# A linear-attention and expert kernel: the table of row numbers is built in SBUF by one-hot matmuls instead of by scatters to DRAM

## The chip, the cores and the metric

The kernel runs on one core of one Trainium2 chip. The metric is device time in microseconds (us), smaller is better; the time before is the median of three runs. A profile is one execution recorded by the hardware profiler; its span is shorter than the device time by what lies around it.

## The reference

Two stages follow each other. The first is a recurrence over 768 positions for 4 batches and 8 heads of width 48:

```python
for t in range(S):
    state = alpha[:, :, t, :, None] * state + np.einsum('bhd,bhe->bhde', k[:, :, t], v[:, :, t])
    y[:, :, t] = np.einsum('bhd,bhde->bhe', q[:, :, t], state)
```

Its output, as 3072 rows of 384 numbers, goes through a layer of 8 experts, one expert per row, with a gate that lets some rows pass unchanged:

```python
do_compute = x @ w_skip > 0
xc = x[do_compute]
logits = xc @ w_gate
e_idx = np.argmax(logits, axis=1)
probs = softmax(logits)                      # largest one is the weight of the row
for e in range(8):
    mask = e_idx == e
    y[mask] = gate_w[mask, None] * (np.maximum(xc[mask] @ w1[e], 0) @ w2[e])
out = x.copy();  out[do_compute] = xc + y    # w1: 384 x 1024, w2: 1024 x 384
```

## The kernel before, in words

The program has one order of instructions for each engine, written out by hand: what stands earlier in the text is issued earlier on its engine, and an engine waits in order. Engines wait for each other by semaphores where data require it.

**Attention, steps 0 to 23.** The 3072 rows are 24 tiles of 128 (tile i: batch i % 4, positions from 128 * (i // 4)). A pair j is the tiles 2j and 2j + 1. `step(i)` does for tile i, or one tile ahead: `scores` (L328, q times k, of tile i + 1), `turn_k` (L341, transposed k, of tile i + 1, up to tile 19), `causal` (L334, DVE: scores below the mask into `st`), `inter` (L358, q times state), `outer` (L384, k times v for the next state, up to tile 19), `intra` (L367, `st` times v), `rows` (L406 and L415: the output turned into rows, of the tile before), `store` (SP: rows to `out`, of two tiles before). The decays come from two scans per pair on DVE, `suffix` (L282) and `prefix` (L300), two pairs ahead; GpSimd multiplies k and q by them (L311, L307) and scales the state (L399). `inspect` (L318, ScalarE) checks that the decays lie within bounds.

**Routing.** Tiles are taken in groups (`GROUPS`). At the end of a group `logits` (L436) multiplies its outputs by the gate weights, `logits_turn` (L446) transposes, and `route` does on DVE: the row maximum, the difference, which expert and whether the row is on (`mg`, a 0/1 matrix of rows by experts), the exponentials on ScalarE and their sum. `rank` (L496 to L502) counts with triangular matmuls how many rows of the same expert stand before a row. Groups from tile `LATE` = 18 on count downwards from slot 255, the others upwards from 0, so that an expert's 256 slots hold early rows below and late rows above. `slots` picks the rank by `mg`. `tick` advances these small operations a few at a time between the large ones.

**The table.** For each tile `scatter` (L526, an indirect DMA issued by GpSimd) writes, for its 128 rows, row number and exponential sum (8 bytes) to `xs` in DRAM at slot 3072 * expert + rank. `xs` is cleared at step 1 (`clear`). `metas` (L643, SP) reads the first 256 slots of each expert back into SBUF once every scatter has landed. `fetch_rows` (L549, indirect DMA from GpSimd) gathers the 256 rows of an expert from `out` by these numbers. An empty slot holds a number out of bounds and is skipped; the buffer was cleared before.

**Expert 0's first rows.** To begin expert 0 before the last rows are in DRAM, `early_rows` (step 21) reads its table as it stands, step 22 gathers those rows into `xr0`, and the rows from tile 18 on reach expert 0 by matmuls: `slots` makes a one-hot matrix `hot` per late tile (L521), `late_parts` splits the tile's rows into two float parts (L558, L559), and `late_rows` (L566) multiplies the two, summing into the PSUM tile `x01`; `early_turn` adds the gathered ones. `split_x` turns both halves into the float parts that the experts use. `attention_end` holds this order.

**Experts.** For each expert, `up` (L686, four blocks of 36 matmul records in two), `down` twice (L701), `turn` of the next expert's gathered rows (L671) between the two, `put` (L708 and an indirect DMA, L710: rows times gate plus input, written to their place in `out`). Weights come by `fetch` on SP's queue, four DMAs each for w1 and w2, and `split` makes the two float parts of them (ScalarE L618, DVE L620). Gathers run three experts ahead. `must_redo` (expert 5) checks whether the shortcuts held; if not, a general path runs at the end.

Instructions of the late stage take over SBUF and PSUM of the attention stage, each waiting until the tile that it overlays is free.

Of the kernel before, what the change touches and what calls it, by code (L numbers as in the profile page):

```python
# [44 lines left out]
BIG = float(1 << 20)  # L45
OFF = 1 << 20
GMAX = 4
GROUPS = ((0, 4), (4, 8), (8, 12), (12, 16), (16, 18), (18, 21), (21, 23), (23, 24))
LATE = 18
TABLE = 16  # L50
# [12 lines left out]
class Kernel:  # L63
# [12 lines left out]
    def constants_first(self):  # L76
# [3 lines left out]
        dram = self.ctx.enter_context(tc.tile_pool(name="dram", bufs=1, space=DRAM))  # L80
        self.dram = dram
        self.xs = dram.tile([E * N, 2], F32, name="xs")
# [26 lines left out]
    def constants_late(self):  # L109
# [13 lines left out]
        base_i = const.tile([1, E], I32, name="base_i")  # L123
        nc.gpsimd.iota(base_i, pattern=[[N, E]], base=0, channel_multiplier=0)
        self.base_row = const.tile([P, 1, E], BF16, name="base_row")
        nc.gpsimd.memset(self.base_row, 0.0)
        nc.gpsimd.tensor_copy(self.base_row[0:1, 0, :], base_i)
# [5 lines left out]
        self.slot = const.tile([P, NT, 1], U32, name="slot")  # L133
        self.idg = const.tile([P, NT, 2], F32, name="idg")
        nc.gpsimd.iota(self.idg[:, :, 0:1].bitcast(I32).rearrange("p (c b) w -> p c b w", b=B),
                       pattern=[[P, C], [S, B], [0, 1]], base=0, channel_multiplier=1)
# [5 lines left out]
        self.empty = const.tile([E, CAP, 2], F32, name="empty")  # L142
        nc.gpsimd.memset(self.empty, 0.0)
        nc.gpsimd.iota(self.empty[:, :, 0:1].bitcast(I32), pattern=[[0, CAP]], base=OFF, channel_multiplier=0)

    def constants_slots(self):

        nc, const = self.nc, self.const
        slots_i = const.tile([P, P], I32, name="slots_i")
        nc.gpsimd.iota(slots_i, pattern=[[1, P]], base=P, channel_multiplier=0)  # L150
        self.slots1 = const.tile([P, P], F32, name="slots1")
        nc.gpsimd.tensor_copy(self.slots1, slots_i)
# [5 lines left out]
    def clear(self):  # L158

        self.nc.sync.dma_start(out=self.xs.rearrange("(e n) w -> e n w", e=E)[:, :CAP, :].rearrange("e n w -> e (n w)"),  # L160
                               in_=self.empty.rearrange("e n w -> e (n w)"))

    def clear_late(self):

        for i in range(LATE + 3, NT):
            row = self.row(i)
            self.nc.sync.dma_start(out=self.out[row:row + P, :], in_=self.xr0[:, 0, :])
# [1029 lines left out]
```

## Time and profile before

| | |
|---|---|
| Device time, median of 3 | 296.95 us (296.1 to 298.43) |
| Profiled execution: device time | 296.78 us |
| Its span | 295.0 us |
| Busy: PE / DVE / ACT / POOL | 268.8 / 210.0 / 159.4 / 132.4 us |
| Bytes moved by DMA | 55.22 MB |

PE is TensorE, PEld its weight loads, DVE VectorE, ACT ScalarE, POOL GpSimd, SP the engine that issues most DMAs. Times in the profile are counted from the start of the span. "L701" is line 701 of the kernel; names such as `ps_o<-w2h,hh` are output and inputs without buffer numbers. The chain of waits follows the work that ended last back to its releasers; "issue" in it is time in which the profile shows no wait. A matmul in four passes is listed by its records, so counts can be twice those of the text.

### The profile page before, as it was taken

The page shows a single profiled execution, that of the slowest core. Times are in us where ns is not written, and L with a number is a line of the kernel's source. Part 1 is how long each engine was busy: PE and PEld are TensorE (multiplying, and loading weights), DVE is VectorE, ACT ScalarE, POOL GpSimd, SP SyncE. Part 2 cuts the span into 40 slices and gives each one's busy share as a digit, 9 for nine tenths or more (in the row PEclk, how much of TensorE's full clock was granted, in tenths as well). Part 3 has the DMA queues.
Part 4 walks back from the last instruction along what each step waited for, and adds up shares of the span by engine and source line. Part 5 has one row for each costly group of instructions (what it writes and reads, how often), then busy time and mean ns, then how long its engine had stood idle before and what let it go on. Part 6 is the DMA issues. An engine that isn't in the chain of part 4 may idle for free.

```text
span 295.0 us, 7438 instructions
## 1 busy us (share of the span) xinstructions
PE 268.8 (91%) x2933; PEld 246.7 (84%) x2933; DVE 210.0 (71%) x376; ACT 159.4 (54%) x388; POOL 132.4 (45%) x141
## 2 busy tenths in 40 slices
PE   8967999999879989999947999999999999999980
PEld 8856888888758768779926999999999999999980
DVE  7999899898795959853525585785758878585720
ACT  8897657567537547542623364745636366354600
POOL 8847567888767665537134503205050230202011
PEclk9999999999999968999996999999999999999996
DMA  5999999799999924023069728578382865815000
GB/s 171 296 265 269 288 287 280 137 255 166 191 290 274 302 86 107 6 60 81 3 199 339 253 78 300 192 221 296 112 306 78 282 232 180 290 36 224 4 29 19
DMA packets 29690, 55.22 MB, mean 187 GB/s; under 512 B 6600, under 2 KB 13312, under 8 KB 29648
## 3 DMA queue, kind: packets, MB, share of 16 engines
q1 hardware_dynamic: 26704, 49.60, 59.8%
q0 software_dynamic: 2944, 5.07, 4.7%
q8 instruction: 25, 0.41, 0.7%
q14 instruction: 17, 0.14, 0.2%
HBM read 47.80 MB, written 8.50 MB: 191 GB/s over the span
## 4 chain that ended last, share of the span: by engine, by line
PE 76%; DMA 7%; DVE 6%; ACT 4%; issue 3%; POOL 1%; POOLq 0%; SPq 0%; DVEq 0%
PE ps_o L701 21%; PE ps_h L686 21%; PE ps_s L328 7%; PE ps_y L367 6%; PE ps_y L358 4%; PE ps_k L406 4%; PE ps_v L384 3%; DMA xs<-idg,slot 3%; PE ps_k L341 3%; DVE sfx L282 3%; PE ps_n L436 2%; DMA xr<-out_dram,meta 2%; PE ps_x L671 2%; DVE pfx L300 1%; DVE st L334 1%
## 5 line engine op out<-in xcount | busy, mean ns | idle before, releaser
L710 POOL DMA_INDIRECT out_dram<-o,meta x16 | 16.1, 1003 | 98.9 <-DVE o L708 98.3
L690 ACT ACTIVATE hh<-ps_h 128x512 fp32r<-128x512 f32 x32 | 19.1, 598 | 48.0 <-PE ps_h L686 48.0
L701 PE MATMUL ps_o<-w2h,hh 128*128 128x384 f32 x128 | 43.9, 343 | 0.0
L701 PE MATMUL ps_o<-w2l,hh 128*128 128x384 f32 x128 | 43.4, 339 | 0.2 <-DVE w2l L620 0.2
L691 DVE SCALAR_TENSOR_TENSOR hl<-ps_h,hh 128x512 fp32r<-128x512 f32 x32 | 22.1, 691 | 29.6 <-ACT hh L690 29.6
L701 PE MATMUL ps_o<-w2h,hl 128*128 128x384 f32 x128 | 43.1, 337 | 0.0
L334 DVE COPY_PREDICATED st<-mask,ps_s 128x1024 f32<-128x1024 uint8 x24 | 31.6, 1315 | 5.4 <-PE ps_s L328 5.4
L311 POOL TENSOR_TENSOR qk<-qk,sfx 112x512 f32<-112x512 f32 x24 | 28.0, 1183 | 14.1 <-DVE dec L296 2.9
L686 PE MATMUL ps_h<-xh,w1h 128*128 128x256 f32 x192 | 33.7, 284 | 0.4 <-ACT xh L585 0.4
L307 POOL TENSOR_TENSOR qk<-qk,pfx 112x512 f32<-112x512 f32 x23 | 26.8, 1180 | 15.8 <-DVE pfx L300 15.8
L686 PE MATMUL ps_h<-xh,w1l 128*128 128x256 f32 x192 | 33.4, 283 | 0.0
L620 DVE TENSOR_TENSOR w2l<-raw,w2h 128x512 fp32r<-128x512 f32 x48 | 31.4, 683 | 2.7 <-ACT w2h L618 2.7
L620 DVE TENSOR_TENSOR w1l<-raw,w1h 128x512 fp32r<-128x512 f32 x48 | 31.3, 705 | 0.0
L318 ACT ACTIVATE junk<-dec 112x512 bf16<-112x512 f32 x48 | 30.6, 638 | 0.8
L371 ACT COPY xt<-ps_y 112x256 f32<-112x256 f32 x48 | 15.5, 374 | 28.5 <-PE ps_y L367 28.5
L618 ACT CAST w1h<-raw 128x512 fp32r<-128x512 f32 x48 | 26.8, 626 | 5.5 <-DMA raw<-in_w_dram 5.5
L618 ACT CAST w2h<-raw 128x512 fp32r<-128x512 f32 x48 | 27.9, 615 | 2.8 <-DMA out_dram<-x 2.8
L328 PE MATMUL ps_s<-qk 64*128 64x128 f32 (+1 forms) x384 | 28.9, 291 | 0.4 <-POOL qk L307 0.4
L549 POOL DMA_INDIRECT xr<-out_dram,meta x18 | 19.7, 1093 | 21.2 <-issue 10.0
L367 PE MATMUL ps_y<-st,v 128*64 128x128 f32 x384 | 28.2, 280 | 0.9 <-issue 0.9
L300 DVE TENSOR_TENSOR_SCAN pfx<-dec,ps_t 112x1040 f32<-112x1040 f32 (+1 forms) x14 | 28.2, 2011 | 1.2
L686 PEld LDWEIGHTS ps_h<-xh,w1h 128*128 128x128 f32 x192 | 28.0, 191 | 0.5 <-ACT xh L585 0.5
(161 smaller groups left out, 555.0 us busy)
## 6 DMA issues: line engine op xcount, KB each, us to landing
raw<-in_w_dram SPq DMA_DIRECT2D x64, 384.0 KB, 4.8
qk<-in_qk_dram SPq DMA_DIRECT2D x20, 384.0 KB, 9.3
dec<-in_dec_dram SPq DMA_DIRECT2D x24, 198.0 KB, 6.9
v<-in_v_dram SPq DMA_DIRECT2D x12, 384.0 KB, 7.7
out_dram<-x SPq DMA_DIRECT2D x24, 192.0 KB, 6.9
qk<-in_qk_dram SPq DMA_DIRECT2D x8, 192.0 KB, 5.7
out_dram<-xr SPq DMA_DIRECT2D x3, 192.0 KB, 7.4
xs<-idg,slot POOLq DMA_INDIRECT x24, 7.6
```

Source lines behind the costliest of these rows:

```text
L300: nc.vector.tensor_tensor_scan(w["pfx"][:PD, s], w["dec"][:PD, s], self.top[:PD].to_broadcast([PD, s.stop - s.start]), 1.0, ALU.mult, ALU.max)
L307: (eng or self.nc.gpsimd).tensor_tensor(w["qh"][:PD], w["qh"][:PD], w["pfx"][:PD], ALU.mult)
L311: (eng or self.nc.gpsimd).tensor_tensor(w["kh"][:PD], w["kh"][:PD], w["sfx"][:PD], ALU.mult)
L318: self.nc.scalar.activation(out=self.junk[:PD], in_=dec, func=AF.Relu, scale=scale, bias=bias, accum_out=self.odd[:PD, n, i:i + 1])
L328: nc.tensor.matmul(ps[:, h, p * P:(p + 1) * P], lhsT=kh[r, p, :], rhs=qh[r, p, :], start=True, stop=True)
L334: self.nc.vector.copy_predicated(w["st"], self.mask, w["ps"])
L367: nc.tensor.matmul(self.place(i, h, p), lhsT=w["v"][:, o:o + 64], rhs=w["st"][:, h, p * P:(p + 1) * P], start=(i < B and p < 2), stop=(p > ...
L618: nc.scalar.copy(out=hi[:, s], in_=raw[:, s])
L620: eng.tensor_tensor(lo[:, s], raw[:, s], hi[:, s].bitcast(F32), ALU.subtract)
L686: nc.tensor.matmul(ps[:, u, :], lhsT=a[:, k, f * P:(f + 1) * P], rhs=b[:, k, :], start=(n == 0), stop=(n == len(order) - 1))
L691: nc.vector.scalar_tensor_tensor(out=hl, in0=ps, scalar=0.0, in1=hh.bitcast(F32), op0=ALU.max, op1=ALU.subtract)
L701: nc.tensor.matmul(ps, lhsT=a[:, f, js], rhs=b[:, f, :], start=(n == 0), stop=(n == 3 * FT - 1))
```

## The change

The table of row numbers no longer goes through DRAM. Each row gets a one-hot vector of 128 slots (`hots`) and, per expert and half of the slots, six small numbers (`vals`): 1, tile number and position within it, and the exponential sum in three bf16 parts (`facts`). A matmul per tile, hots transposed times vals, summed over tiles, puts them in PSUM at partition = slot: `table`. `ids` makes row numbers of it, with an out-of-bounds number for a slot that does not hold exactly one row.

- `scatter`, `clear`, `metas` and `gates` go, with their constants. `sums` and `marks` make `facts`, `hots` and `vals`: on GpSimd for the groups ending at 4, 8, 12 and 16 (seven operations at each odd step, `run_jobs`), on DVE (the sums on GpSimd) for tiles 16 to 19, and on GpSimd for the late groups at the end.
- The late part starts at tile 20, not 18: groups are 0-4, 4-8, 8-12, 12-16, 16-20, 20-23 and 23-24.
- Ranks and slots of an early group stand right after `scores` and `turn_k`, ahead of the scans of the step; before, they came after `inter`, behind the scans.
- `early_rows` (step 21) multiplies the 20 early tiles' table and gathers expert 0's early rows at once. `early_turn` moves from `attention_end` to the start of step 23. Late stores need not wait for that gather any more (`apart`).
- `late_table` runs after expert 0's first up block: the four late tiles' table is added, row numbers and gates of all experts are made, and the gathers of experts 1, 0 and 2 follow.
- Buffers for gathered rows exist from the start and are cleared at steps 15, 21 and 22; `clear_late` moves from step 14 to 17 and covers four tiles. `inspect` runs three tiles ahead, not four. The order at the end of the attention is another.

The diff, cut to its core:

```diff
-GROUPS = ((0, 4), (4, 8), (8, 12), (12, 16), (16, 18), (18, 21), (21, 23), (23, 24))
-LATE = 18
+GROUPS = ((0, 4), (4, 8), (8, 12), (12, 16), (16, 20), (20, 23), (23, 24))
+LATE = 20
...
-        for i in range(LATE + 3, NT):
+        for i in range(LATE, NT):
...
+    def sums(self, g, eng):
...
+        yield eng.tensor_copy(part(3), w["sum"])
+        yield eng.tensor_tensor(rest[:, :, 0:1], w["sum"], part(3), ALU.subtract)
+        yield eng.tensor_copy(part(4), rest[:, :, 0:1])
+        yield eng.tensor_tensor(part(5), rest[:, :, 0:1], part(4), ALU.subtract)
+
+    def marks(self, g, eng, eng_hot):
...
+            yield eng.tensor_scalar(out=up, in0=w["s"], scalar1=float(P), scalar2=None, op0=ALU.is_ge)
+            yield eng.tensor_scalar(out=s, in0=up, scalar1=-float(P), scalar2=None, op0=ALU.mult)
+            yield eng.tensor_tensor(s, s, w["s"], ALU.add)
+            yield eng.tensor_tensor(half[:, :, 1, :], mg, up.to_broadcast([P, n, E]), ALU.mult)
+            yield eng.tensor_tensor(half[:, :, 0, :], mg, half[:, :, 1, :], ALU.subtract)
...
+        for t in range(n):
+            yield eng_hot.tensor_scalar(out=hots[:, t, :], in0=slots, scalar1=s[:, t, :], scalar2=None, op0=ALU.is_equal)
...
+        yield eng.tensor_tensor(vals.rearrange("p t j e w -> p t (j e) w"), mg.unsqueeze(3).to_broadcast(shape),
+                                self.facts[:, g0:g1, :].unsqueeze(2).to_broadcast(shape), ALU.mult)
+
+    def table(self, groups, ps):
+
+        tiles = [(self.grp[g0], t) for g0, g1 in groups for t in range(g1 - g0)]
+        for n, (w, t) in enumerate(tiles):
+            self.nc.tensor.matmul(ps, lhsT=w["hots"][:, t, :], rhs=w["vals"][:, t].rearrange("p j e w -> p (j e w)"),
+                                  start=(n == 0), stop=(n == len(tiles) - 1))
+
+    def ids(self, out, tab):
...
+        nc.vector.tensor_scalar(out=b, in0=col(0), scalar1=1.0, scalar2=float(OFF), op0=ALU.not_equal, op1=ALU.mult)
+        nc.vector.scalar_tensor_tensor(out=a, in0=col(1), scalar=float(P), in1=col(2), op0=ALU.mult, op1=ALU.add)
+        nc.vector.tensor_tensor(out, a, b, ALU.add)
...
     def early_rows(self):
...
-        self.meta0 = self.late.tile([P, NB, 2], F32, name="meta0")
-        ins = nc.sync.dma_start(out=self.meta0, in_=self.slot_rows(0))
-        self.after(ins.ins, "xs")
-        self.early = [ins.ins.name]
+        ps = self.bank[:, P + 32 * GMAX:][:, 0:NB * E * TABLE]
+        self.table([g for g in GROUPS if g[0] < LATE], ps)
+        self.rowtab = self.late.tile([P, NB, E, TABLE], F32, name="rowtab")
+        nc.scalar.copy(out=self.rowtab.rearrange("p j e w -> p (j e w)"), in_=ps)
+        first = self.late.tile([P, NB, 1], U32, name="first")
+        self.ids(first, self.rowtab[:, :, 0:1, :])
+        for ins in self.fetch_rows(self.xrb[0], first):
+            self.apart(ins.ins, "first rows", "late rows")
...
+    def late_table(self):
+
+        nc = self.nc
+        ps = self.ps_f.tile([P, E * TABLE], F32, name="ps_f")
+        self.table([g for g in GROUPS if g[0] >= LATE], ps)
+        tab = self.rowtab
+        top = tab[:, 1].rearrange("p e w -> p (e w)")
+        nc.vector.tensor_tensor(top, ps, top, ALU.add)
+        self.row_of = self.late.tile([P, NB, E], U32, name="row_of")
+        self.ids(self.row_of, tab)
...
@@ step
-        if i == 14:
+        if i == 17:
             self.clear_late()
...
-        if i == LATE + 1:
+        if i in (15, LATE + 1, LATE + 2):
+            self.clear_rows(max(0, i - LATE))
+        if i == LATE:
             self.splits = self.split(0, "w1", nc.vector)
...
+        done = ends.get(i - 2)
+        ranked = done and done[1] < LATE
         if i + 1 < NT:
             self.scores(i + 1)
             self.turn_k(i + 1)
+            if ranked:
+                self.tick(99)
+                self.rank(done)
             self.causal(i + 1)
+        if ranked:
+            self.finish_group(done)
...
+        if t == 1 or i >= LATE:
+            self.run_jobs(7 if i < LATE - 1 else 99)
+        g = ends.get(i)
+        if i == NT - 1:
+            self.x_tiles(0)
+            self.early_turn()
+            self.split_x(0, 0, self.early_x)
+        if g and i >= LATE:
+            self.logits(g)
         self.inter(i)
+        if i == LATE + 1:
+            self.early_rows()
+        if g and i >= LATE:
+            self.logits_turn(g)
+            self.small = self.route(g)
+            self.tick(4)
...
         self.outer(i)
...
+        self.intra(i)
+        if i == LATE:
+            self.rank(g)
             self.tick(99)
-            self.todo += range(*done)
-        self.intra(i)
...
+            self.finish_group(g)
+            self.run_jobs(99)
...
@@ attention_end
+        first, last = GROUPS[-2:]
+        self.rank(first)
+        self.rows(a)
+        for _ in self.slots(first):
+            pass
+        self.logits_one(b)
+        self.late_high(a)
+        self.tick(99)
+        for _ in chain(self.sums(first, nc.gpsimd), self.marks(first, nc.gpsimd, nc.gpsimd)):
+            pass
+        self.rows(b)
...
+        self.late_low(a)
         self.late_rows(LATE)
+        self.rank(last)
+        self.late_rows(LATE + 1)
+        self.late_rows(a)
+        for _ in self.slots(last):
+            pass
+        self.late_high(b)
+        self.late_low(b)
+        next(route)
+        self.late_rows(b)
+        self.split_x(0, 1, self.x01)
...
@@ experts
-        self.metas((1, 0))
         for _ in self.fetch(1, "w1"):
             pass
-        self.metas(range(2, E))
-        for e in (1, 0, 2):
-            self.gather(e)
...
                 self.up(e, g)
+                if (e, g) == (0, 0):
+                    self.late_table()
+                    for n in (1, 0, 2):
+                        self.gather(n)
                 advance(split, 3)
```

More of the change, by code (lines that the diff above doesn't have):

```diff
@@ L178, in disjoint, with apart @@
         self.scatters.setdefault(group, []).append(ins.name)
+    def apart(self, ins, own, other):
+        self.tc.declare_no_dep(ins, group=other, reason="the early rows and the late rows")
+        self.tc.add_to_no_dep_group(own, ins)
     def after(self, ins, group):
@@ L418, in store @@
         row = self.row(i)
-        self.nc.sync.dma_start(out=self.out[row:row + P, :], in_=self.work[i]["x"])
+        ins = self.nc.sync.dma_start(out=self.out[row:row + P, :], in_=self.work[i]["x"])
+        if i >= LATE:
+            self.apart(ins.ins, "late rows", "first rows")
     def tick(self, n=1):
@@ L451, in logits_one @@
         nc = self.nc
-        bank = self.ps_s.tile([P, 2, HW], F32, name="ps_s")[:, 0, :]
+        bank = self.end[:, 0, :]
         for m in range(NP):
@@ L552, in fetch_rows, with late_high @@
             bounds_check=N - 1, oob_is_err=False) for j in range(NB)]
-    def late_parts(self, i, eng):
+    def late_high(self, i):
         w = self.work[i]
-        hi, lo = w["parts"] = [self.lp.tile([P, DM], F32R, name=f"late{n}{i}") for n in "hl"]
-        self.nc.scalar.copy(out=hi, in_=w["x"])
-        eng.tensor_tensor(lo, w["x"], hi.bitcast(F32), ALU.subtract)
+        w["parts"] = [self.lp.tile([P, DM], F32R, name=f"late{n}{i}") for n in "hl"]
+        self.nc.scalar.copy(out=w["parts"][0], in_=w["x"])
@@ L595, in weight_pools @@
         self.xx = pool("xx", 2)
+        self.late = pool("late", 1)
+        self.xrb = [self.late.tile([P, NB, DM], F32, name=f"xr{i}") for i in range(3)]
         self.wt, self.ew = {}, {e: {} for e in range(E)}
@@ L1050, in step, with finish_group, run_jobs @@
             self.carry(j)
-        for n in (i + 2, i + 4) if i < 2 else (i + 4,):
+        for n in (i + 2,) if i < 4 else (6, 7) if i == 4 else (i + 3,):
             if n < NT:
                 self.inspect(n)
-        if g and g[0] < LATE:
+        if g and i < LATE:
             self.logits_turn(g)
-            self.small = chain(self.small, self.route(g))
-        done = ends.get(i - 1)
-        if done and done[1] >= LATE:
-            self.tick(99)
-            self.rank(done)
-            self.small = self.slots(done)
-        for _ in range(1 if i < LATE else 2 if i < NT - 1 else 3):
-            if self.todo:
-                self.scatter(self.todo.pop(0))
-        if done and done[1] >= LATE:
-            self.todo += range(*done)
-        self.tick(99 if t or i >= LATE else 1)
+            self.small = self.route(g)
+        if i < LATE:
+            self.tick(99 if t else 3)
+    def finish_group(self, g):
+        for _ in self.slots(g):
+            pass
+        last = g[1] == LATE
+        eng = self.nc.vector if last else self.nc.gpsimd
+        self.jobs = chain(self.jobs, self.sums(g, self.nc.gpsimd), self.marks(g, eng, eng))
+    def run_jobs(self, n):
+        for _ in range(n):
+            next(self.jobs, None)
     def scan_right(self, j):
```

221 lines of the change are left out of this document (86 added, 135 removed).

## The prediction

> **What bounds the kernel now.** I read the page's slices first, for the clock.
>
> ```profile
> PEclk9999999999999968999996999999999999999996
> ```
>
> TensorE runs at full clock except in two places, about 105 to 116 us and 155 to 162 us. Both lie where work changes hands, so next I read the chain of waits in order of time (start, length, what):
>
> ```profile
> 50.78 1.01 PE ps_n L436 x32
> ...
> 69.12 1.01 PE ps_n L436 x32
> ...
> 94.39 1.09 PE ps_s L328 x16
> 95.48 0.53 PE ps_k L341 x4
> 96.01 0.60 PE ps_y L358 x16
> 96.61 0.54 PE ps_v L384 x13
> 97.15 0.98 PE ps_y L367 x15
> ...
> 101.10 1.24 DVE st L334
> 102.33 2.20 DVE sfx L282
> ...
> 104.67 1.07 PE ps_n L436 x16
> ...
> 106.97 1.81 PE ps_s L328 x16
> ...
> 130.65 0.86 PE ps_s L454 x8
> ...
> 132.04 1.39 PE ps_v L566 x12
> ...
> 138.50 9.63 DMA xs<-idg,slot
> 148.32 2.39 DMA meta<-xs
> ...
> 152.91 4.90 DMA xr<-out_dram,meta
> ...
> 158.75 4.92 PE ps_o L701 x24
> 163.68 8.63 PE ps_h L686 x72
> 172.31 4.17 PE ps_o L701 x24
> 176.48 0.66 PE ps_x L671 x6
> ...
> 181.30 8.63 PE ps_h L686 x72
> ```
>
> Three stages are to be seen. Up to step 17 the chain is TensorE's own: four steps from one logits block (50.78) to the next (69.12) take 18.34 us, and the rows of one step (scores 1.09, `turn_k` 0.53, inter 0.60, outer 0.54, intra 0.98, `rows`, four transposes like `turn_k`, 0.53) give 4 x 4.27 + 1.01 = 18.1. Nothing there but TensorE's own work counts. In steps 18 and 19 the chain goes over DVE: causal copy, the 2.20 us scan, then logits at 104.67. And from 138.50 to 158 it leaves the engines: last scatter, table read back, gather. From 163.68 an expert takes 181.30 - 163.68 = 17.62 us of TensorE without a gap; this the change does not touch. The timeline gives the two points between which the changes lie (start, length, engine, line):
>
> ```profile
> 98.56 1.16 PE L328 MATMUL ps_s<-qk 64*128 64x128 f32 x16
> ...
> 136.95 0.72 PE L686 MATMUL ps_h<-xh,w1h 128*128 128x256 f32 x3 [0.35 <-ACT xh L585]
> ...
> 139.50 0.60 ACT L690 ACTIVATE hh<-ps_h 128x512 fp32r<-128x512 f32 x1 [2.27 <-PE ps_h L686]
> ```
>
> Step 18 begins at 98.56 (scores of tile 19), expert 0 at 136.95.
>
> **The hole in expert 0.** From 136.95 to expert 1's start at 163.68 are 26.73 us, against 17.62 for an expert: 9.1 us are lost. They contain the wait for expert 1's rows and the half clock after it (down block 4.92, not 4.17). The change removes its cause: no scatter (9.63), no read-back (2.39). In their place, after the first of four up blocks of expert 0, TensorE does four small table matmuls and DVE one sum and three index operations. Let U be the start of expert 0. The first block's `hh` starts at U + 2.55 (139.50 - 136.95) and takes 0.60. For what DVE and GpSimd do I take these group rows (busy us, then mean ns):
>
> ```profile
> L311 POOL TENSOR_TENSOR qk<-qk,sfx 112x512 f32<-112x512 f32 x24 | 28.0, 1183 | 14.1 <-DVE dec L296 2.9 <-DVE sl L511 2.5 <-DMA qk<-in_qk_dram 2.0
> L526 POOL DMA_INDIRECT xs<-idg,slot x24 | 24.5, 1021 | 5.3 <-issue 4.4 <-DVE st L334 0.3 <-DVE on L478 0.3
> L399 POOL TENSOR_TENSOR state<-state,sfx 112x384 f32<-112x384 f32 x8 | 7.2, 896 | 0.0
> L152 POOL CAST slots<-slots_i 128x128 f32<-128x128 int32 x1 | 0.3, 291 | 0.1
> L127 POOL CAST base_row<-base_i 1x8 bf16<-1x8 int32 x1 | 0.2, 179 | 0.1
> L559 DVE TENSOR_TENSOR latel<-x,lateh 128x384 fp32r<-128x384 f32 x6 | 3.2, 552 | 2.2 <-ACT lateh L558 2.2
> L521 DVE TENSOR_SCALAR hot<-slots,s 128x128 fp32r<-128x128 f32 x6 | 1.7, 371 | 0.1
> L477 DVE TENSOR_TENSOR ps_t<-ps_n,mx 128x32 f32<-128x32 f32 x4 | 0.8, 188 | 0.0
> ```
>
> DVE's `hl` of that block costs some 0.7 (L559 scaled from 384 to 512 columns), so DVE is free for the table at U + 3.9; four small operations at 0.19 give U + 4.7. Two gather issues at 1.02 (L526's kind) put the second at U + 5.7, and with the 4.90 of the chain its rows are there at U + 10.6. TensorE needs them at U + 8.63 + 4.17 = 12.8. That is 2.2 us of slack, so I take the whole 9.1 back. Late inputs are possible: the table matmuls wait for GpSimd's marks of the last tile, which can begin after the exponent sum of tile 23, about 1.1 us before U (six late matmuls at 0.116, below, and the wait of 0.35): four small operations (0.18 each), a hot matrix (0.29) and a product (under 0.4), 1.4 us, so U + 0.3, and TensorE asks only at U + 2.2. SP's queue no longer holds expert 1's first weights behind the table's read-back; they load while expert 0's ups run. Stores of the last two tiles no longer queue behind the early gather (`apart`).
>
> **Steps 18 to U.** The wait to go is that of the logits at step 18, and the clock after it; the wait row, and stretches of 4 us (from:to, length, busy time of PE, PEld, DVE, ACT, POOL; then clock, DMA share, GB/s):
>
> ```profile
> PE ps_n L436 <- DVE sl L511: 2.1, 1, 2.1
> ```
>
> ```profile
> 104.00:108.00 4.00, 3.33 (x33) 2.86 (x35) 1.46 (x8) 1.52 (x5) 3.17 (x3) 0.71 0.01 2
> 108.00:112.00 4.00, 4.00 (x49) 3.17 (x48) 3.18 (x9) 2.14 (x6) 1.11 (x2) 0.50 0.56 152
> 112.00:116.00 4.00, 4.00 (x65) 3.37 (x63) 3.97 (x6) 2.83 (x9) 1.91 (x2) 0.94 0.66 144
> ```
>
> Logits waited 2.1 us for `slots` of the former group, which DVE did behind the scan. The clock then cost 4 x 0.29 + 4 x 0.50 + 4 x 0.06 = 3.4 us (scores 1.81 for 1.09). In the changed order ranks and slots stand ahead of the scan, and no group ends at 18, so both go: 5.5 us. What is late next is the late part itself, so I lay TensorE's queue out anew from 98.56:
>
> - Work: 5 scores x 1.09 = 5.45; 8 `turn_k` and `rows` x 0.53 = 4.24; 6 inter x 0.60 = 3.60; 2 outer x 0.54 = 1.08; 6 intra x 0.98 = 5.88; 2 logits x 1.01 = 2.02; `logits_one` 0.86; six transposes of the early rows 0.66 (L671); late rows, now 4 tiles x 6 = 24 matmuls (36 before), at 1.39 / 12 = 0.116: 2.78; early table, 20 matmuls, new. Its 128x96 bf16 form has no row. Bounds: nothing, if it hides in waits for DVE, and twice L566's 0.116; I take 0.116, a matmul with its own 128x128 weights: 2.3. Three ranks and two logit transposes: 1.2, an estimate from the same 0.116. Sum 30.1.
> - Wait in step 20. Its group now ends there (16 to 20), so `logits_turn`, route, rank and marks run inside the step. ScalarE's copy of the logits stands in order behind the check of tile 22 and two weight casts:
>
> ```profile
> L318 ACT ACTIVATE junk<-dec 112x512 bf16<-112x512 f32 x48 | 30.6, 638 | 0.8
> L618 ACT CAST w1h<-raw 128x512 fp32r<-128x512 f32 x48 | 26.8, 626 | 5.5 <-DMA raw<-in_w_dram 5.5
> ```
>
>   2 x 0.64 + 2 x 0.63 = 2.5, which begin only after the output copies of tile 19 (about 0.7 by the same rate); 3.2 against scores, logits and inter, 2.7, is a wait of 0.5 at least. The checks' read-outs stand there too; I take 1.2.
> - Wait in step 21. The table matmuls need DVE's marks for tiles 16 to 19: two sums, two slot operations and five small ones at 0.19, four hot matrices at 0.37, a product of 384 columns at 0.55: 3.8, against scores and inter, 1.7. TensorE waits 2.1; causal copy 22 and two weight splits on DVE stand behind the marks.
> - Wait in step 23. `early_turn` now stands ahead of everything in that step. From the table's start DVE needs 1.24 + 2 x 0.7 + 3 x 0.19 = 3.2 to the indices, GpSimd issues the second gather 1.3 later, at 4.5. TensorE reaches `early_turn` after 2.3 + 0.53 + 0.98 + 3.2 (step 22) = 7.0. Landings of the two early gathers before:
>
> ```profile
> DMA to landing us min/median/max: 2.5/3.1/3.6
> ```
>
>   With 2.5 it waits for nothing, with 4.90 for 2.4: I take 1.0.
> - Before the first up block 0.4, as in the row at 136.95.
>
> Together 30.1 + 4.7 = 34.8, U = 133.4, 3.6 us earlier than 136.95. Without waits U would be 129.1; all ends bad (gather 4.90, table 0.23 each) 137.1.
>
> **Steps 0 to 17.** 24 scatters of 1.02 leave GpSimd. A group of four tiles there gets 14 jobs: four exponent parts, three small ones and two halves at 0.18, four hot matrices at 0.29, a 384 product at 0.90: 3.7, against 4.1 for its four scatters. Per 18.34 us GpSimd also does eight scalings at 1.18 and two states at 0.90, 11.2; the sum 14.9 fits, so TensorE's chain hides it and I take nothing. What that cover costs if it is gone is a rival below. DVE is not loaded more (one small route operation less); the later checks of `inspect` move ScalarE work that no row of the chain shows there. Clearing of late rows moves from step 14 to 17, four stores for three, behind the last loads on SP.
>
> At this price row and rule differ: 384 columns of two inputs cost 0.90 on GpSimd and 0.55 on DVE. The Trainium skill (GPSIMD Engine Reference, Engine selection) speaks against the move: elementwise work belongs on VectorE, GpSimd being about twice as slow for two inputs. The trace agrees in direction, at 1.6. By twice DVE's rows the 14 jobs cost 2 x (9 x 0.19 + 4 x 0.37 + 0.55) = 7.5, an estimate, over the 7.1 left: 0.4 us a group, 1.6 in all, and the forecast would be 285.7, short of a reversal.
>
> **Sum.** The profiled execution took 296.78 (span 295.0 and 1.8 around it), 0.17 under the median of 296.95. 296.78 - 9.1 - 3.6 = 284.1.
>
> **Rivals.**
> 1. The late part gives the front's gain back. The new waits of 2.1 and up to 2.4 are as long as the one that was followed by half clock; one such stretch costs 3.4 (287.5), with the bad ends 3.7 more (291.2). For: the marks on DVE and the order of step 23 put both waits on TensorE's queue. Against: the waits are split by work. The Trainium skill (TensorE: Matmul & The Clock Gate, What's actually happening) has the clock fall only after an idle window of about 3.4 us. The trace does not bear that out: 2.1 us were enough here. By that rule something else slowed 105 to 113, and would stay: a loss of 3.4 that I counted as gained, 287.5 again. Chance 0.22.
> 2. The hole is only half closed: marks or gather late by more than the slack of 2.2. Half of 9.1 left gives 288.7; all but 2 us left, 291 to 293. For: last tile, table, gather and turn are one chain. Against: 138.50 to 150.7 was the scatter and its read-back, and both are gone. Chance 0.10.
> 3. Slower: GpSimd becomes the bound in steps 6 to 19. No row shows its `is_equal` against a per-partition value or a product with stretched bf16 operands. If a job costs as much as an indirect issue (1.02), 14 cost 14.3, with 11.2 that is 25.5 per 18.34 us: 7.2 x 4 groups = 29 us, 313. It decides from 7.1 / 14 = 0.51 per job, and cancels the gain at (7.1 + 3.2) / 14 = 0.73. Against: 0.18 to 0.29 in the nearest rows. Chance 0.06.
> 4. Better than forecast: the table hides in waits and no wait costs: 279.7. Chance 0.05.
>
> **Numbers.** The forecast, 284.1, has 0.57, its own range 280.5 to 287. The range of 8 in 10 takes in rival 1 and the half-closed hole: 280.5 to 291; left out are rival 3, the bad end of 2, and 4, some 0.16. A measurement of this kernel can tell about 1% (3 us) from no change. Faster by over 1% (under 294) are the forecast and rivals 1, 2 and 4, 0.94, less 0.06 for 1 and 2 falling together: 0.88; within 1%: those 0.06; slower, rival 3: 0.06.
>
> **What would show it.** Hole: between the first up block and expert 1's no TensorE gap above 1 us, 17.6 to 18.5 us from U to expert 1; wrong if a wait for `xr` or the table stays. Front: U near 133.4, no wait of logits for `slots`, clock 1.00 in 104 to 113, and waits of some 2 us ahead of the table matmuls and 0 to 2 ahead of `early_turn`; U above 137 is rival 1. GpSimd: jobs of 0.2 to 0.9, four steps still 18.3; a longer period there is rival 3. The prediction falls if steps 0 to 17 change by over 2 us.

## The result, and the profile after

The changed kernel takes 282.87 us (median of 4, 281.75 to 284.91) against 296.52 us (295.6 to 298.43) for the kernel before: a ratio of 0.954, 95% interval 0.946 to 0.962. The profiled execution took 282.12 us, with a span of 280.4 where the kernel before had 295.0. So 14.6 us of the span went, 13.7 by the medians; forecast were 12.7. Medians here are over all runs of a kernel; ratios and their intervals leave out the runs that fell in a slower state at a lower clock.

The points at which the stages begin, as starts of matmuls in the timeline (scores of step 18; first up of expert 0, the U of the prediction; first up of expert 1), tell where:

| from, to | before, us | after, us | gain | forecast |
|---|---|---|---|---|
| start to step 18 | 98.56 | 96.18 | 2.4 | 0 |
| step 18 to U | 38.39 | 36.07 | 2.3 | 3.6 |
| U to expert 1 | 26.57 | 18.06 | 8.5 | 9.1 |
| expert 1 to the end | 131.5 | 130.1 | 1.4 | 0 |

The chain of waits of the changed kernel in order of time (start, length, what) answers to the chain shown of before:

```profile
102.56 2.33 POOL qk L303 x2
...
107.18 3.06 POOL hots L549 x4
110.24 0.80 POOL vals L551
111.05 2.28 POOL qk L299 x2
...
118.78 1.30 POOL xr L586
...
120.38 2.94 DMA xr<-out_dram,first
...
132.25 2.52 PE ps_h L728 x18
134.77 0.12 PE ps_f L558 x4
134.88 6.56 PE ps_h L728 x54
141.44 4.17 PE ps_o L743 x24
145.62 0.66 PE ps_x L713 x6
```

From U on it is TensorE's alone. The late table (`ps_f`) costs 0.12 us, and the transposes of expert 1's rows come at 145.62 without a wait: no scatter, no read-back, no gather is left there. But between step 18 and U the chain now runs over GpSimd, from the k scalings at 102.56 to the q scalings that end at 113.33, and on through its first jobs for tiles 16 to 19, a wait for VectorE's row numbers and the early gather, which lands at 123.32. TensorE's waits in 104 to 134 us (total, times, longest) are:

```profile
PE ps_s L320 <- POOL qk L299: 2.0, 1, 2.0
PE ps_s L619 <- DVE latel L601: 0.9, 1, 0.9
PE ps_n L440 <- ACT pl L433: 0.7, 1, 0.7
PE ps_v L621 <- DMA xr<-out_dram,first: 0.6, 1, 0.6
PE ps_h L728 <- ACT xh L628: 0.4, 1, 0.4
PE ps_n L492 <- DVE on L473: 0.2, 1, 0.2
PE ps_n L558 <- DVE vals L551: 0.2, 1, 0.2
```

The 2.0 us for `qk` stand ahead of the scores at 112.23, are counted in step 20, and are new. (The row for `latel` can't be told from a wait for the early gather: that operation ends at 122.19, and the first half of the rows, issued at 118.78, lands 3.4 us later, at 122.2. L619 reads these rows.) Stretches of 4 us, columns as in the prediction:

```profile
108.00:112.00 4.00, 1.94 (x26) 1.46 (x24) 3.42 (x13) 2.04 (x7) 4.00 (x5) 1.00 0.14 51
112.00:116.00 4.00, 3.56 (x52) 2.97 (x52) 3.83 (x10) 1.46 (x4) 3.59 (x8) 0.71 0.01 2
116.00:120.00 4.00, 4.00 (x59) 3.26 (x57) 3.67 (x8) 2.92 (x7) 1.22 (x1) 0.87 0.16 52
```

The half clock is not gone; it moved from 105 to 113 us to the stretch behind the new wait, 4 x 0.29 + 4 x 0.13 = 1.7 us lost. At half clock that is 3.4 us long. The Trainium skill (TensorE: Matmul & The Clock Gate, What's actually happening) has the gate decide over windows of about 3.4 us, which agrees with that length; but TensorE worked for 1.94 of the 4 us ahead of it, and its longest wait was 2.0, so a whole idle window was not needed here either. Whether a wait of this length brings half clock depends on where it falls; the last section shows it.

Two group rows (busy us, mean ns) show GpSimd's new work at its real price (the first mean is of fifteen at 0.59 to 0.62 us and one at 1.32):

```profile
L549 POOL TENSOR_SCALAR hots<-slots,sr 128x128 bf16<-128x128 bf16 x16 | 10.1, 647 | 0.0
L551 POOL TENSOR_TENSOR vals<-half,facts 128x384 bf16<-128x384 f32 x4 | 3.3, 833 | 0.0
```

### The profile page after: what moved, and what is told of

Its sections match the earlier page's. It is cut to its first block, busy times and chain, and to the rows that moved or that the text cites. A ratio compares the mean times of both kernels' runs of the same rounds, so it can differ in the third digit from the quotient of the medians.

```text
span 280.4 us, 7410 instructions
## 1 busy us (share of the span) xinstructions
PE 262.3 (94%) x2934; PEld 242.2 (86%) x2934; DVE 211.1 (75%) x371; ACT 158.8 (57%) x385; POOL 133.7 (48%) x189
## 4 chain that ended last, share of the span: by engine, by line
PE 78%; DVE 6%; POOL 5%; ACT 4%; issue 3%; DMA 2%; POOLq 0%; DVEq 0%
PE ps_h L728 25%; PE ps_o L743 24%; PE ps_y L359 6%; PE ps_s L320 6%; PE ps_v L376 3%; PE ps_k L398 3%; PE ps_y L350 3%; DVE sfx L274 3%; PE ps_k L333 3%; PE ps_n L430 2%; ACT junk L310 2%; PE ps_x L713 2%; POOL hots L549 1%; DMA xr<-out_dram,first 1%; DVE st L326 1%
## 5 line engine op out<-in xcount | busy, mean ns | idle before, releaser
L752 POOL DMA_INDIRECT out_dram<-o,row_of x16 | 16.1, 1005 | 99.5 <-DVE o L750 99.2
L743 PE MATMUL ps_o<-w2l,hh 128*128 128x384 f32 x128 | 42.8, 335 | 0.0
L320 PE MATMUL ps_s<-qk 64*128 64x128 f32 (+1 forms) x384 | 28.1, 285 | 3.4 <-POOL qk L299 3.4
L665 DVE TENSOR_TENSOR w1l<-raw,w1h 128x512 fp32r<-128x512 f32 x48 | 30.3, 685 | 0.0
L320 PEld LDWEIGHTS ps_s<-qk 64*128 64x128 f32 (+1 forms) x384 | 23.5, 188 | 7.1 <-POOL qk L299 3.9
L274 DVE TENSOR_TENSOR_SCAN sfx<-dec,ps_t 112x1041 f32<-112x1041 f32 (+2 forms) x14 | 28.0, 1999 | 0.4 <-DMA dec<-in_dec_dram 0.4
L728 PE MATMUL ps_h<-xl,w1h 128*128 128x256 f32 x192 | 28.2, 283 | 0.0
```

The source lines that it names most:

```text
L274: self.nc.vector.tensor_tensor_scan(w["sfx"][:PD, s][:, ::-1], w["dec"][:PD, s][:, ::-1], self.top[:PD].to_broadcast([PD, s.stop - s.start ...
L320: nc.tensor.matmul(ps[:, h, p * P:(p + 1) * P], lhsT=kh[r, p, :], rhs=qh[r, p, :], start=True, stop=True)
L665: eng.tensor_tensor(lo[:, s], raw[:, s], hi[:, s].bitcast(F32), ALU.subtract)
L728: nc.tensor.matmul(ps[:, u, :], lhsT=a[:, k, f * P:(f + 1) * P], rhs=b[:, k, :], start=(n == 0), stop=(n == len(order) - 1))
L743: nc.tensor.matmul(ps, lhsT=a[:, f, js], rhs=b[:, f, :], start=(n == 0), stop=(n == 3 * FT - 1))
```

## The experiments

All were run against the kernel before. The stages in their traces, in us; the time of a step runs from the start of one step's scores to the next's:

| kernel | step 18 | steps 18, 19, 20, 21 | U | expert 1 | span |
|---|---|---|---|---|---|
| before | 98.56 | 8.05, 6.60, 3.24, 5.47 | 136.95 | 163.52 | 295.0 |
| before, again | 97.06 | 7.64, 4.55, 4.91, 8.12 | 146.42 | 167.12 | 298.0 |
| e1: rank first, alone | 96.97 | 6.14, 3.89, 5.36, 8.34 | 140.91 | 161.19 | 292.1 |
| the change | 96.18 | 4.38, 3.71, 7.96, 5.80 | 132.25 | 150.31 | 280.4 |
| e2: rank back | 95.21 | 4.46, 3.71, 7.89, 5.61 | 131.78 | 149.82 | 280.2 |
| e3: table later | 97.15 | 4.39, 3.71, 7.92, 5.25 | 134.92 | 154.83 | 284.6 |
| e4: jobs behind | 95.93 | 4.39, 3.71, 7.32, 7.50 | 132.16 | 151.17 | 281.4 |
| e5: hots on VectorE | 98.12 | 5.52, 3.71, 10.42, 6.76 | 137.11 | 155.35 | 285.2 |
| e6: clears earlier (its longest run) | 98.87 | 4.39, 3.70, 7.98, 5.66 | 138.30 | 156.34 | 286.2 |
| e7: e4 and e5 | 98.82 | 5.53, 3.71, 8.49, 6.53 | 135.66 | 153.86 | 284.5 |
| e10: e4, splits later | 97.04 | 4.38, 3.71, 4.62, 9.35 | 132.90 | 150.93 | 280.7 |
| e9: room for the route | 96.15 | 4.38, 3.71, 5.34, 5.35 | 131.40 | 149.43 | 279.3 |
| e11: e9, turn later | 97.10 | 4.38, 3.71, 5.33, 5.35 | 129.71 | 147.74 | 277.6 |

**The order of the ranks alone.** The kernel before, with only rank and slots put ahead of the scans:

```
+        done = ends.get(i - 2)
+        ranked = done and done[1] < LATE
         if i + 1 < NT:
             self.scores(i + 1)
             self.turn_k(i + 1)
+            if ranked:
+                self.tick(99)
+                self.rank(done)
             self.causal(i + 1)
+        if ranked:
+            for _ in self.slots(done):
+                pass
+            self.todo += range(*done)
...
-        if done and done[1] < LATE:
-            self.tick(99)
-            self.rank(done)
-            self.small = self.slots(done)
...
-        if done and done[1] < LATE:
-            self.tick(99)
-            self.todo += range(*done)
```

> The kernel before with one part of the change alone: ranks and slots of an early group right after scores and turn_k, ahead of the scans; scatters, groups and everything else as before. My theory (logits of step 18 waited 2.1 us for slots behind a scan, and the half clock after it cost 3.4 us): steps 18 and 19 shrink from 14.65 us to 9 or 10, clock 1.00 from 104 to 113 us, 5.5 us off the time, 291. Rival (the clock fell for another reason, as an idle window of 3.4 us would be needed): 2 us off at most, 294.5 to 295, and the half clock stays.

It took 295.79 us, a ratio of 0.994 (0.986 to 1.001). Steps 18 and 19 fell from 14.65 to 10.03, as expected, and steps 20 and 21 rose from 8.71 to 13.70. With the wait of the logits the half clock behind it went, as it should if that wait was its cause; there is half clock again behind the next wait of 2 us:

```profile
104.00:108.00 4.00, 4.00 (x78) 3.34 (x74) 3.24 (x13) 3.03 (x11) 3.75 (x3) 1.00 0.82 172
108.00:112.00 4.00, 2.32 (x40) 1.67 (x36) 3.97 (x5) 3.97 (x12) 2.57 (x3) 1.00 0.52 150
112.00:116.00 4.00, 3.64 (x36) 3.01 (x36) 4.00 (x6) 1.31 (x3) 3.53 (x4) 0.58 0.10 32
```

The longest waits of TensorE from step 18 on:

```profile
PE ps_n L446 <- ACT pl L439: 2.2, 1, 2.2
PE ps_n L446 <- issue: 2.1, 1, 2.1
PE ps_s L328 <- POOL qk L307: 2.0, 1, 2.0
```

So a wait taken away in step 18 came back as others from two steps later on, and U was 4.0 us later. In its turn the hole in expert 0 was 20.28 us where it had been 26.57, and TensorE waits for no gathered row in it: expert 0's up blocks took 11.45 us instead of 8.63, at half clock. By the ratio this edit alone is worth 1.9 us, with the interval from 4.1 to none; 5.5 was expected of it.

**The change without that order.** Rank goes back behind the inter products, slots behind the scan:

```
-            if ranked:
-                self.tick(99)
-                self.rank(done)
             self.causal(i + 1)
-        if ranked:
-            self.finish_group(done)
...
+        if ranked:
+            self.tick(99)
+            self.rank(done)
+            self.finish_group(done)
```

> The changed kernel with ranks behind inter and slots behind the scans again, as before. Theory A (the new groups suffice: no group ends at 18, so no logits wait for those slots): 282 to 284, same as the change. Theory B (the order is what matters): the wait and the half clock come back, 3 to 5.5 us more, 286 to 288.5.

282.88 us, 0.951 (0.945 to 0.957): the same as the change, with the same steps. In the change it is enough for steps 18 and 19 that no group of logits ends at 18 any more. The order of the ranks adds nothing to it.

**The slack of the gather.** The late table stands behind the third up block, not the first:

```
-                if (e, g) == (0, 0):
+                if (e, g) == (0, 2):
                     self.late_table()
```

> The changed kernel with the late table after the third up block of expert 0 instead of the first, 4.3 us later. My theory (the hole is the wait of expert 1's turn for its gathered rows, and the change left some 2.3 us of slack): TensorE waits 2 us ahead of that turn, 284.9. Rival (the turn would wait for something else anyway, or the gather is not what closes the hole): no wait, 282.9.

285.87 us, 0.962 (0.957 to 0.967). From U to expert 1 it is 19.91 us, 1.85 more, and the wait shows:

```profile
PE ps_x L713 <- DMA xr<-out_dram,row_of: 1.7, 1, 1.7
```

Put off by 4.3 us, the gather is 1.7 late, so by this run it has 2.6 us to spare in the change; the prediction had 2.2. The figure depends on how long the gather takes: its second half took some 4.8 us to land here (issued at 145.44, waited for until 150.26) and 3.1 in the trace of the change, where the rows were there at 141.56 and TensorE took them from 145.46 on, 3.9 us later. (U itself was later in this trace by 2.7. Step 18 accounts for 1.0 of it; the rest lies in steps ahead of the edit, with a longer wait for the early gather, 1.5 and 0.8 us, and half clock behind that one.)

**GpSimd's jobs behind the scalings.** In step 19 seven small jobs stay ahead, and the halves, hot matrices and product go behind the scalings and the carry:

```
-            self.run_jobs(7 if i < LATE - 1 else 99)
+            self.run_jobs(7 if i < LATE else 99)
...
             self.carry(j)
+            if i == LATE - 1:
+                self.run_jobs(99)
```

> The changed kernel; in step 19 seven of the fourteen GpSimd jobs of tiles 12 to 15 stand ahead of the scalings of q as in other steps, and the rest (hot matrices, product) behind scalings and state. My theory (the 2.0 us wait of scores for q in step 20 and the half clock from 113.8 to 117 us come from hot matrices of 0.77 us each ahead of the scaling): both go, 3.5 us off, 279 to 280. Rival (the wait only moves to the early table's matmuls, as DVE's marks end at 115.8 anyway): at most 1 us off, 282.

282.12 us, 0.949 (0.945 to 0.954). The scores no longer wait for `qk`, so GpSimd's queue was the cause of that wait; but the rank and the table wait instead, 2.8 us together. The first of the waits is VectorE's: its two split subtractions, ahead of the route, took 2.78 us beside GpSimd's scalings.

```profile
PE ps_n L492 <- DVE on L473: 1.7, 1, 1.7
PE ps_n L558 <- DVE vals L551: 1.1, 1, 1.1
```

```profile
107.71 2.78 DVE L665 TENSOR_TENSOR w1l<-raw,w1h 128x512 fp32r<-128x512 f32 x2
```

**The hot matrices on VectorE**, which is faster at them: alone, and with the former edit.

```
-        self.jobs = chain(self.jobs, self.sums(g, self.nc.gpsimd), self.marks(g, eng, eng))
+        self.jobs = chain(self.jobs, self.sums(g, self.nc.gpsimd), self.marks(g, eng, self.nc.vector))
```

> The changed kernel with the four hot matrices of each early group built by VectorE (0.19 us each in the trace for the group that it builds) where GpSimd took 0.77 each in step 19. Theory (a): GpSimd's queue is what delays the q scalings, so they start some 3.1 us earlier in step 19, the scores of step 20 wait nothing for them (2.03 before), the half clock behind that wait goes or shrinks, and the last up of expert 0 starts 2.0 to 3.0 us earlier: 279.9 to 281.0 us. Rival (b): VectorE is late in the same steps (its small operations took 1 us while GpSimd scaled), so that the rank and the late table wait instead by as much: 282 to 283 us, with the scores' wait gone but waits for VectorE of 1.5 us or more in steps 20 to 22.

> Both edits: the hot matrices of the early groups on VectorE, and of GpSimd's work in step 19 seven small operations ahead of the scalings and the rest behind them. Theory (a): the values of the early table are ready 2.4 us sooner than with the second edit alone, so the table's wait of 1.1 us goes, the 1.7 us for the rank stays or shrinks: 280.0 to 281.5 us. Rival (b): the rank's wait is VectorE's and grows by the 0.8 us of the hot matrices: 281.5 to 283 us.

Both came out slower than the change, and than either of my theories allowed: 287.14 us, 0.968 (0.959 to 0.976), and 285.67 us, 0.962 (0.955 to 0.968). The intervals touch that of the change; the traces show where the time goes. Steps 10, 14 and 18, which the theories left out, take 5.01, 5.55 and 5.52 us in the first where the change has 4.38, 4.39 and 4.38. And in step 19 the timeline of the first shows:

```profile
109.33 0.74 DVE L549 TENSOR_SCALAR hots<-slots,sr 128x128 bf16<-128x128 bf16 x4 [2.96 <-POOL sr L544]
...
110.37 2.32 DVE L292 TENSOR_TENSOR_SCAN pfx<-dec,ps_t 112x1040 f32<-112x1040 f32 x1
```

```profile
112.77 2.32 POOL L299 TENSOR_TENSOR qk<-qk,pfx 112x512 f32<-112x512 f32 x2 [2.01 <-DVE pfx L292]
```

VectorE takes 0.74 us for the four, but first waits 2.96 for GpSimd's `sr`, with the scan behind it in its queue; and GpSimd then waits 2.01 for that scan. Two queues now wait for each other in turn. In the second the matrices run beside the scalings and take four times as long:

```profile
110.13 3.17 DVE L549 TENSOR_SCALAR hots<-slots,sr 128x128 bf16<-128x128 bf16 x4
```

**The clears, earlier again.** To test the 2.4 us of steps 0 to 17:

```
-        if i == 17:
+        if i == 14:
             self.clear_late()
...
-        if i in (15, LATE + 1, LATE + 2):
+        if i in (12, LATE + 1, LATE + 2):
```

> The changed kernel with the clears of the late rows and of the first gather buffer put three steps earlier (steps 14 and 12), about where the kernel before had them. Theory (a): the 2.4 us that steps 0 to 17 gained came from moving these clears away from the steps that load much: two steps between 14 and 17 get 1 to 2.5 us longer than 4.24 and the time is 284 to 285.5 us. Rival (b): the stretched steps of the kernel before were chance stalls of that one execution (its relative with only the rank moved had none of that size): steps 14 to 17 stay at 4.24, 4.39, 4.24, 5.36 and the time at 282 to 283 us.

283.91 us over its five runs, 281.45 over the three that make the ratio of 0.946 (0.937 to 0.956). As the table counts steps, the four in question (14 to 17 in the expectation) are 13 to 16, and they stay at 4.24, 4.38, 4.24 and 5.36: the clears are not it.

**The kernel before, a second trace.**

> The kernel before once more, for a second trace of it. If its steps 14 and 16 were stretched by its own work (the stores of the clears), they are again 1 us and more above 4.24 and step 18 starts at 98 to 99 us. If they were chance stalls, they are at 4.2 to 4.6, and step 18 starts at 96 to 97 us as in the changed kernel, or other steps are stretched. The hole in expert 0 and its 26.6 us to the up of expert 1 stay in any case.

One run took 299.71 us. As the table counts steps, those stretched in the first trace (14 and 16 in the expectation) are 13 and 15: 5.50 and 6.68 us, where the change has 4.24 in both. Neither was here (4.23 and 4.24); step 8 was, to 6.73. Step 18 began at 97.06. So the stretches are not the kernel's own in every run; what stalls it is not shown. But the hole did not stay as I had expected: 20.70 us, and the steps from 18 to U took 49.36 instead of 38.39. Again TensorE waits for no gathered row in the hole. The chain of that trace holds three pieces that the profile can give to no engine of the core:

```profile
119.57 2.15 another core or an unknown queue
...
131.32 2.27 another core or an unknown queue
...
156.69 2.04 another core or an unknown queue
```

What waits in each is ScalarE, for a result of TensorE whose last record lies some 2 us back: the logits end at 119.99 and 131.11 and the copies of them begin at 121.73 and 133.61, the last up block ends at 156.78 and its `hh` begins at 158.75. So TensorE's result or its signal came late; why, no run settled. One such piece (1.68 us at 118.45) is in the chain of the kernel with the ranks first, none in the first trace of before, and none in any kernel without the scatters.

**Room for the route.** From these: the splits of expert 0's first weight leave step 20, first on the kernel with the jobs behind, then on the change itself together with five jobs in step 18, where GpSimd was idle for 1.32 us, and one q scaling on VectorE.

```
-        for _ in range(4):
-            next(self.splits, None)
+        if LATE < i < NT - 1:
+            for _ in range(4):
+                next(self.splits, None)
...
             self.split_x(0, 0, self.early_x)
+            for _ in range(4):
+                next(self.splits, None)
```

and, in the second only:

```
         if t == 0 and i > 0 and j + 2 < NJ:
+            if i == LATE - 2:
+                self.run_jobs(5)
             self.scan_right(j + 2)
...
-                    self.scale_q(2 * j + 4 + n)
+                    self.scale_q(2 * j + 4 + n, nc.vector if i == LATE - 1 and n == 0 else None)
```

> The kernel with the jobs behind the scalings (seven ahead) and the splits of expert 0's first weight one step later, without the other two edits. Theory (a): the 1.7 us that the rank waited there for VectorE was the two split subtractions ahead of the route, 2.78 us of VectorE's time beside GpSimd's scalings where two take 1.33 alone; both waits (0.7 and 1.7) go, step 20 falls from 7.32 to about 5, but the table then waits up to 2 us for the values that GpSimd ends at about 114: 280.3 to 281.5 us. Rival (b): the table's wait takes all of it: 281.8 to 282.8 us.

> The changed kernel with three edits in steps 18 to 23: the splits of expert 0's first weight start in step 21 and end in step 23 (not 20 to 22), so that neither ScalarE nor VectorE has them ahead of the router of step 20; five of the GpSimd jobs stand ahead of the k scalings of step 18, where GpSimd was idle for 1.32 us; and one of the two q scalings of step 19 is VectorE's. Theory (a): steps 20 and 21 are long because GpSimd's jobs and the splits stand ahead of the route (0.73 for pl, 2.03 for the scores, and the half clock behind them); with them out of the way step 20 falls from 7.96 to 5 to 5.5, step 21 to 4.5 to 5.5, no half clock at 112 to 118, and the last up of expert 0 starts 2.5 to 4 us earlier: 278.5 to 280.5 us. Rival (b): the table of the early tiles then waits for GpSimd's values (ready at 109.7) or VectorE's (113.5 by the sums of the last tile), and the splits in step 23 delay the first part of expert 0: 281 to 283 us.

The first: 281.52 us, 0.946 (0.942 to 0.949). Step 20 fell to 4.62, and step 21 rose to 9.35, as the table waited 3.5 us for GpSimd's values and VectorE's:

```profile
PE ps_n L558 <- POOL vals L551: 2.3, 1, 2.3
PE ps_n L558 <- DVE vals L551: 1.2, 1, 1.2
```

The second: 280.78 us, 0.945 (0.940 to 0.950). Steps 20 and 21 fell to 10.69 from 13.76, and no half clock was left at 112 to 118. Of these 3.1 us only 0.8 reached U; the rest went into a longer wait for the early gather in step 23, and half clock behind it:

```profile
PE ps_s L619 <- DMA xr<-out_dram,first: 1.5, 1, 1.5
PE ps_v L621 <- DMA xr<-out_dram,first: 0.7, 1, 0.7
```

```profile
120.00:124.00 4.00, 3.29 (x30) 2.69 (x31) 1.81 (x3) 1.51 (x3) 0.00 (x0) 0.61 0.03 9
```

**And the turn later.** In step 23 of that kernel `x_tiles`, `early_turn` and `split_x` go behind the last `intra`, the last splits behind the route:

```
-        if i == NT - 1:
-            self.x_tiles(0)
-            self.early_turn()
-            self.split_x(0, 0, self.early_x)
...
+            if i == NT - 1:
+                for _ in range(4):
+                    next(self.splits, None)
...
         self.outer(i)
         self.intra(i)
+        if i == NT - 1:
+            self.x_tiles(0)
+            self.early_turn()
+            self.split_x(0, 0, self.early_x)
```

> The kernel with room for the route, and in step 23 the early turn stands behind the last logits, inter and intra (1.0, 0.6, 0.24 and 1.0 us of matmuls) instead of ahead of them; the last splits stand behind the route. Theory: what was left of the loss was the early gather, for which TensorE waited 1.5 and 0.7 us with a half clock behind it (0.61 in 120 to 124); with 2.9 us of other matmuls ahead of the turn both waits and the half clock go, and the last up of expert 0 starts 2 to 3 us sooner: 278 to 279.3 us. Rival: the turn and the late rows then stand in the chain of the last groups (route, ranks, hot matrices), which takes the wait over: 280.3 to 281.5 us, U within 0.7 us of 131.4.

280.51 us (278.48 to 281.8), 0.948 (0.943 to 0.953), with a profiled execution of 279.3. The waits for the gather are gone, the clock is full, and from step 18 to U it takes 32.61 us against 36.07 in the change:

```profile
116.00:120.00 4.00, 3.87 (x65) 3.00 (x68) 3.96 (x9) 3.31 (x8) 2.60 (x3) 1.00 0.35 108
120.00:124.00 4.00, 4.00 (x67) 3.35 (x62) 1.71 (x7) 1.95 (x7) 0.69 (x1) 1.00 0.21 64
```

The trace shows a gain of 3.5 us in that stage. Of the times, the medians of this kernel and the one ahead of it (280.5 and 280.8) lie some 2 us under the change's 282.9; they stem from separate comparisons. By their ratios the four kernels with the jobs or the splits moved (0.949, 0.946, 0.945 and 0.948) can't be told from each other, and their intervals overlap that of the change (0.946 to 0.962) as well. So the gain of these last edits is shown in the traces, not by the times.

## Why the prediction was right, and where it was not

**The sum.** 284.1 was forecast, 282.87 measured, inside the own range of the likeliest case. The mechanism was the one named: the scatters and their read-back left the path, and the gather fits into expert 0's work. In all three traces with the scatters GpSimd issues the first gather of expert 1 at about the same time, 151.55, 150.79 and 148.61 us, whether U is 136.95, 146.42 or 140.91; in the change it does so at 137.04, 4.8 us behind U.

**The hole.** 9.1 forecast, 8.5 in the two traces; 18.06 us from U to expert 1 lies in the 17.6 to 18.5 of the prediction. The step behind it, a slack of 2.2 us, is borne out by the late table (2.6). What the prediction did not see is that the hole was not a quantity of its own. The scatters end at a time of theirs, so what the front loses the hole gives back: in the second trace of before the front is 11.0 us longer and the hole 5.9 shorter, and with the ranks first the hole shrinks to 20.28. What is left of it there is half clock and a late result of TensorE, not the gather. Only both together can be laid to the change: 64.96 from step 18 to expert 1 in the first trace (70.06 in the second), 54.13 after it, 10.8 us where the two terms made 12.7. How much of the longer fronts of the other two traces, with their late results and half clock, belongs to the scatters stays open.

**Steps 18 to U.** 34.8 forecast, 36.07 measured. The wait for `slots` went, but for one of the two reasons given: without the order of the ranks the time is the same. Of the new waits (4.7 forecast, 0.7 + 0.2 + 2.0 + 0.2 + 0.9 + 0.6 + 0.4 = 5.0 measured) the sum was right by luck. The table's 2.1 was 0.2, because TensorE came 2.0 late to it, and the 1.2 for `pl` was 0.7; `early_turn`'s 1.0 was 1.5. The 2.0 for the q scalings was in no term, nor the 1.7 of half clock behind it, which the sum left to rival 1.

**The term that failed** is the price of a job on GpSimd. A hot matrix was put at 0.29, by a cast of the same size; it takes 0.60 in the earlier groups, and in step 19 three take 0.60 to 0.62 and one 1.32. With its nine small operations and the product (0.83, forecast 0.90), 14 jobs ran from 104.83 to 111.01, 6.2 us, not 3.7. The 7.5 that I weighed was nearer, but it doubled every job, and the rule of the Trainium skill (GPSIMD Engine Reference, Engine selection) is twice for two inputs and about the same rate for one. Doubling only the operations with two inputs, the same rows give 9 x 0.19 + 5 x 0.19 + 4 x 0.37 + 2 x 0.55 = 5.2, an estimate; of the hot matrices, which have one, the trace does not bear the rule out (0.60 against 0.19 on VectorE, four in 0.76). In steps 0 to 17 this cost nothing, as the prediction had it, since four steps have 7.1 us of room on GpSimd (they take 18.2 after the change). But the cover was argued as a sum over four steps, and in step 19 it is the place that counts: the jobs stand ahead of scalings for which the next scores wait.

**Rivals.** The first came true in part: a new wait of 2 us with half clock behind it, in step 20 instead of 21 or 23, at 3.7 us in all. Part of that is chance: with the table later the same wait of 2.0 stood there, and no half clock followed. The rule of a whole idle window, by which the half clock of before would have stayed, does not hold here: with the ranks first it went with the wait, and TensorE had worked 1.31 of the 3.4 us ahead of it (last section). The hole was not half closed, and GpSimd did not become the bound of the periodic steps.

**Steps 0 to 17.** Taken as nothing, they gained 2.4, past the 2 us at which the prediction was to fall. By the second trace of before and the one with the ranks first (step 18 at 97.06 and 96.97), 1.5 of these were stalls that the first trace alone has; the change and the kernels that edit nothing in it ahead of step 18 start it at 95.9 to 97.2. So the term stands within what one trace can tell.

**The end.** From the end of the last write's issue to the end of the span it is 5.7 to 6.3 us in the three traces with scatters and 4.6 to 5.5 in the others. I had no term for it, and nothing was tried on it: open.

## What to carry to other kernels

A hole behind a transfer is not a fixed sum: whatever is gained ahead of it, the transfer takes back until it is itself off the path, so price both together and take a second trace before splitting them. When work moves to an engine with room, ask not only whether the sum fits but what stands behind it in that engine's queue, at the one place where somebody waits; an in-order queue that waits for another engine in the middle (the hot matrices on VectorE) can cost more than the slower engine. And once the first wait is gone, follow it: here it went from the scalings to the table to the gather, and by the traces only the third edit let the gain through.

## What the hardware showed that was not expected

VectorE and GpSimd stop each other. In the change, two small VectorE operations took 1.03 and 1.11 us while GpSimd scaled (0.17 and 0.16 in the kernel with the splits later, where it did not), each ending with one of GpSimd's two instructions:

```profile
111.01 2.32 POOL L299 TENSOR_TENSOR qk<-qk,pfx 112x512 f32<-112x512 f32 x2
```

```profile
111.18 1.03 DVE L543 TENSOR_SCALAR sr<-up 128x4 f32<-128x4 f32 x1
112.24 1.11 DVE L544 TENSOR_TENSOR sr<-sr,s 128x4 f32<-128x4 f32 x1
```

Four hot matrices took VectorE 0.76 us with GpSimd idle or small, and 3.17 beside the scalings. The Trainium skill (SBUF — State Buffer, Who interferes with whom) states such a lock: the two engines share a pair of ports, and whoever has it keeps it for a whole instruction. The traces agree, down to the end of the instruction. It fits the split subtractions of 2.78 us in the kernel with the jobs behind, too, and GpSimd's hot matrix of 1.32 in step 19: it runs from 108.34 to 109.66, beside the two split subtractions on VectorE (107.95 to 109.28), and with the matrices behind the scalings and these subtractions, in that same kernel, all four take 0.60 to 0.62.

The half clock comes in pieces of 3.4 us: in the change it lasts from 113.7 to 117.1, in the kernel before from 105.7 to 112.5, twice that, and with the ranks first from 133.1 to 146.7, four times. Counted in such pieces, what decides is how long TensorE works within one of them:

| kernel | piece, us | TensorE busy, us | clock in the next piece |
|---|---|---|---|
| before | 102.3 to 105.7 | 1.31 | 0.50 |
| the change | 110.3 to 113.7 | 1.47 | 0.50 |
| e2: rank back | 108.2 to 111.6 | 1.17 | 0.50 |
| e9: room for the route | 117.5 to 120.9 | 1.27 | 0.50 |
| e3: table later | 108.4 to 111.8 | 2.17 | 1.00 |
| e3: table later | 111.8 to 115.2 | 2.03 | 1.00 |

The wait for the q scalings is 2.0 us in the change and 2.0 in e3 (111.1 to 113.2). In the change it lies within one piece; in e3 (pieces counted back from its own half clock, 125.5 to 128.9) the border at 111.8 cuts it in two, and the clock stays full. So the same wait costs 1.7 us more in one run and nothing in another. Where the limit lies is not settled: 1.81 us of work was followed by half clock in e4 (109.4 to 112.8) and 1.68 was not with the ranks first (126.3 to 129.7).
